# Four interleaved layers on one core: later, two-deep weight loads and a new order for all engines

## The chip, the cores and the metric

One core of a Trainium2 chip runs the kernel. The metric is device time in microseconds of one execution, the median of several runs. TensorE (PE) multiplies, PEld is its weight load, VectorE (DVE), ScalarE (ACT) and GpSimd (POOL) do the elementwise work, SyncE (SP) issues nearly all DMAs.

## The reference

Four layers on x of 2048 tokens by 448 channels: attention A, gated MLP B, A, B, with the same weights in both rounds, bf16 at the ends.

```python
def _A_ref(x, wqkv, wo):            # H=16, Dh=28, W=8, dil=2
    q, k, v = qkv of x @ wqkv
    idx = pos[:, None] - off[None, :]          # the token and 7 before it, 2 apart
    logits = einsum("bhsd,bhswd->bhsw", q, k[idx]) * Dh ** -0.5   # idx < 0 masked
    return softmax(logits) weighted v[idx], heads joined, @ wo
def _B_ref(x, w_gate, w_up, w_down):
    return ((x @ w_gate) * (x @ w_up)) @ w_down                   # F = 1792
x = x + _A_ref(_layernorm(x)); x = x + _B_ref(_layernorm(x))
x = x + _A_ref(_layernorm(x)); x = x + _B_ref(_layernorm(x))
```

## The kernel before

**Tiling.** Tokens lie in 16 blocks of 128, even tokens in blocks 0 to 7 and odd ones in 8 to 15, so that the dilated window becomes a plain one. Layers 0 and 2 are attention, 1 and 3 the MLP. Each layer is cut into chunks of 256 or 512 tokens (`ACH`, `BCH`), and `SEQ` interleaves the chunks of neighbouring layers. All weights are loaded once and stay in SBUF.

**An attention chunk.** Statistics and normalization of a block (`bn`, `mv`, `lnv`, `rstd`, `xn`), then its transposition into `xnTa` (`T`), by TensorE and a copy (`Tps`, in the chunks of `PE_T`) or by a DMA transposition that SP issues. Then the projections into q and k (`qk_chunk`, lines 363 and 740), v (`v_group`), scores (`S`, line 850), `Exp` on ACT (line 857), mask on DVE (line 867), attention times v (`AV`, line 887), normalization and the output projection with `wo` (`Y`). Four of the 16 heads' v goes through DRAM: the projection's spare columns are written to `vt` (SP, line 749) and read back with a DMA transposition (line 760); `vones` fills the rows of ones there.

**A projection unit** is two pieces: in the first, each half of the PE rows works for one of two outputs, in the second the halves are exchanged. The second waits, with a semaphore that TensorE itself raises, for the first to be through (`crossed`, `selfd`). Other pieces may stand between the two.

**An MLP chunk.** Normalization and a DMA transposition into `xnTb` (line 639), 14 gate/up units (`Gps`, `Ups`; each contracts over 7 tiles of 64 channels and depends on all 14 weight tiles `wg` 0 to 6 and `wu` 0 to 6 in `WGU`), the product (lines 978 and 981) and the down projection with `WD` (`Dd`).

**Mixed bursts.** The small matmuls of `S` and `AV` use a part of the PE rows and columns. In the order's text an entry such as `547+415@24.40` puts strips of another, large product (the host) into the burst at the places given.

**The order.** Nothing is decided at run time. `Sched.add` numbers every operation, with its engine choices, dependences and an estimated duration; `ORD` then gives, for each engine, the whole list of operation numbers, and `BANK` the PSUM banks of each. The lists were made by a planner that knew the estimates (`lat` of a DMA: `GUL` for gate and up tiles, `WOL` for wo, `WDL` for the down weights), but `lat` itself has no effect in the built kernel; the dependences and the order do. An engine waits for an operation's semaphores at its place in the list, and everything behind it on this engine waits too. SP is one such list: a DMA that must wait for another one's landing holds up all SP's later DMAs.

**Loads before.** SP issues in order: blocks 0 and 1 of x, two staged parts of wqkv, blocks 2 and 3, the second quarter of x, the third, two tiles of `WV`, the fourth quarter, two small staged tiles (`stv`, the v columns that go into the spare columns of WQK: `wqp`), the four `wo` tiles (line 570), then the chain of bulk weights (`link`): each entry depends on the landing of the entry `DEPTH` places before it, so three are in flight. The chain begins behind the second, third and fourth quarters of x, and goes through the 14 gate/up tiles, `vones` and the four parts of `WD`. Within it stand the transpositions of blocks 14 and 15 of layer 0, behind `wg` 4. ACT issues the other two staged parts of wqkv. The eight staged pieces are copied into `WQK` (`wqk`, line 552): five by POOL, three by ACT. POOL builds the masks `MK` with small selects (line 522) before, between and behind its copies.

The rest of the order around these loads: TensorE warms up on zeros, transposes blocks, projects chunk 0 (q, k), the first v, chunk 1, and so on; the first gate/up unit is its operation 303, and behind the attention chunks the MLP of layer 1 begins, while layer 0's last chunks go on.

Of the kernel before, what the change touches and what calls it, by code (L numbers as in the profile page):

```python
# [22 lines left out]
FC = F // 128  # L23
# [24 lines left out]
GUL = 4000.0  # L48
DEPTH = 3
WOL = 14000.0  # L50
WDL = 3500.0
# [347 lines left out]
def build(nc, A_x, A_wqkv, A_wo, B_w_gate, B_w_up, B_w_down, out):  # L399
# [88 lines left out]

    load_x(0, 0, 1, "d_x0", 3400.0)
    load_x(0, 1, 2, "d_x0b", 4250.0)  # L490
    load_stage("act", 0, 3650.0)
    load_stage("act", 2, 5650.0)
    load_stage("sp", 1, 5850.0)
    load_stage("sp", 3, 6450.0)
    load_x(0, 2, 4, "d_x0h", 7050.0)
    load_x(1, 0, 4, "d_x1", 8300.0)
    load_x(2, 0, 4, "d_x2", 9500.0)
    for a in range(2):
        head_dma("sp", WV[:, 2 * a:2 * a + 2, :], wv_rows(a, 2 * D, 3 * D), ("wv", a), "d_wv", (9650.0, 10850.0)[a])
    load_x(3, 0, 4, "d_x3", 12000.0)  # L500
    for a in range(2):
        head_dma("sp", stage[:, SV + 2 * a * DH * VT:SV + 2 * (a + 1) * DH * VT].rearrange("p (b n) -> p b n", b=2), wv_rows(a, 2 * D + VD, 3 * D), ("stv", a), "d_stv", (11500.0, 12400.0)[a])
    sc.add("act", one(act_table_load), 1650.0, prio=-9900)

    def memset(eng, ap, val, key, est):
        sc.add(eng, one(lambda E: E.memset(ap, val), key), est, prio=-40)

    memset("dve", warm, 0.0, "c_warm", 700)
    memset("dve", eps_sb[:], EPS, "c_eps", 70)
    memset("dve", wo_g[:], 0.0, "c_wo", 1000)  # L510
    sc.add("pool", one(lambda E: E.memset(ident[:], 1.0), "i_id"), 600, prio=-46)
    sc.add("pool", one(lambda E: E.affine_select(ident[:], ident[:], [[-1, 128]], ALU.is_equal, 0.0, base=0, channel_multiplier=1), "c_id"), 300, deps=["i_id"], prio=-46)
# [52 lines left out]
    ones_dst = vt_all.rearrange("(t e) (a n) -> t e a n", e=32, n=128)[:, DH:32]  # L565
    ones_src = ones32[0:32, :].unsqueeze(1).to_broadcast([32, 16, 128])
    for j in range(4):
        dst = wo_g[32 * j:32 * j + DH, :, :]
        src = A_wo.rearrange("(c j e) d -> j e c d", c=4, j=4, e=DH)[j]
        head_dma("sp", dst, src, ("wo", j), "d_wo", WOL, deps=["c_wo"])  # L570
    chain = [("x", -1, 4), ("x", -1, 8), ("x", -1, 12)]

    def link(dst, src, key, sem, lat, deps=()):
        plain_dma("sp", dst, src, key, sem, deps=[chain[-DEPTH], *deps], lat=lat)
        chain.append(key)

    for k in range(7):
        for w, W_ in enumerate((B_w_gate, B_w_up)):
            link(WGU[64 * w:64 * w + 64, k, :], W_[64 * k:64 * k + 64, :], (("wg", "wu")[w], k), f"d_w{'gu'[w]}{k}", GUL)
    link(ones_dst, ones_src, ("vones",), "d_one", WDL, ["c_ones"])  # L580
    for n in range(4):
        f0, f1 = (0, 4, 7, 11, 14)[n:n + 2]
        link(WD[:, f0:f1, :], B_w_down[128 * f0:128 * f1, :].rearrange("(c p) e -> p c e", p=128), ("wd", n), f"d_wd{n}", WDL)
    WDR = [("wd", n) for n in range(4)]
    WO = [("wo", j) for j in range(4)]

# [10 lines left out]
    readersA = {}  # L597
# [110 lines left out]
    def qk_chunk(li, j, prio):  # L708
# [35 lines left out]
        for B in range(c0 // 128, c1 // 128):  # L744
            readersA.setdefault((li, B), []).extend([("Kps", li, j, 3), ("Qps", li, j, 3)])
# [378 lines left out]
```

## Time and profile before

| | before |
|---|---|
| time, median of 3 runs | 384.17 us (384.14 to 384.42) |
| the profiled execution's own time | 383.78 us |
| its span, first to last instruction | 382.0 us |
| granted TensorE clock, mean | 1.00 |
| DVE, ACT, POOL busy share | 70%, 53%, 3% |
| DMA | 22.75 MB, mean 60 GB/s, 272 GB/s in the first slice |
| landing of a gate tile, an up tile (median) | 4.8, 3.5 us |

How to read it: an instruction row gives start and length in us, engine and line, the tiles written and read, the count, and in brackets the idle time of the engine ahead of it with what ended it. `SPq` and `ACTq` are DMA issues; the length is the issue's, the landing comes later. In a row by stages the columns are the stretch, its length, and the busy time of PE, PEld, DVE, ACT and POOL, then the clock, the DMA engines' share and GB/s. Matmuls are pipelined: their rows overlap, and the time that a group holds TensorE is the distance to the next group's start.

### The profile page before, as it was taken

The page shows a single profiled execution, that of the slowest core. Times are in us where ns is not written, and L with a number is a line of the kernel's source. Part 1 is how long each engine was busy: PE and PEld are TensorE (multiplying, and loading weights), DVE is VectorE, ACT ScalarE, POOL GpSimd, SP SyncE. Part 2 cuts the span into 40 slices and gives each one's busy share as a digit, 9 for nine tenths or more (in the row PEclk, how much of TensorE's full clock was granted, in tenths as well). Part 3 has the DMA queues.
Part 4 walks back from the last instruction along what each step waited for, and adds up shares of the span by engine and source line. Part 5 has one row for each costly group of instructions (what it writes and reads, how often), then busy time and mean ns, then how long its engine had stood idle before and what let it go on. Part 6 is the DMA issues. An engine that isn't in the chain of part 4 may idle for free.

```text
span 382.0 us, 14245 instructions
## 1 busy us (share of the span) xinstructions
PE 376.1 (98%) x6406; PEld 211.2 (55%) x6406; DVE 266.5 (70%) x588; ACT 204.3 (53%) x401; POOL 10.1 (3%) x41
## 2 busy tenths in 40 slices
PE   7999999999999999999999999999999999999997
PEld 4556587544555445445566787544455544445764
DVE  6984989996787576786758765764767686454413
ACT  5999976746645773235554555366455453134310
POOL 7110000000000000000000000000000000000000
PEclk9999999999999999999999999999999999999999
DMA  8877532500360044013201115310422004120003
GB/s 272 224 163 204 94 76 47 87 6 2 64 80 15 17 75 64 3 27 61 42 3 29 36 25 90 62 29 9 70 46 22 27 2 94 40 62 2 2 2 108
DMA packets 55615, 22.75 MB, mean 60 GB/s; under 512 B 46132, under 2 KB 54660, under 8 KB 55556
## 3 DMA queue, kind: packets, MB, share of 16 engines
q1 hardware_dynamic: 54868, 21.34, 28.0%
q8 instruction: 50, 0.82, 0.9%
q10 hardware_dynamic: 688, 0.52, 0.4%
q14 instruction: 9, 0.07, 0.1%
HBM read 8.54 MB, written 2.71 MB: 29 GB/s over the span
## 4 chain that ended last, share of the span: by engine, by line
PE 92%; ACT 4%; DVE 1%; DMA 1%; SPq 0%; issue 0%
PE ps L363 84%; PE ps L850 2%; PE ps L366 2%; PE ps L887 2%; PE ps L993 1%; ACT qk L740 1%; DMA x_sb<-in_A_x_dram 1%; DVE st L615 1%; ACT xnTa L654 1%; ACT E_sb L857 0%; SPq L460 0%; ACT R_sb L914 0%; ACT v_sb L832 0%; DVE qk L740 0%; ACT R_sb L913 0%
## 5 line engine op out<-in xcount | busy, mean ns | idle before, releaser
L363 PE MATMUL ps<-xnTb,WGU 64*128 64x512 bf16 (+1 forms) x1914 | 174.2, 333 | 0.0
L363 PEld LDWEIGHTS ps<-xnTb,WGU 64*128 64x128 bf16 x1914 | 93.2, 94 | 70.2 <-issue 0.5
L978 ACT ACTIVATE g_sb<-ps 128x512 bf16<-128x512 f32 (+1 forms) x140 | 69.0, 510 | 84.9 <-PE ps L363 76.9
L981 DVE TENSOR_TENSOR hT<-g_sb,ps 128x512 bf16<-128x512 bf16 (+1 forms) x140 | 77.0, 575 | 51.1 <-ACT g_sb L978 48.5
L363 PE MATMUL ps<-WD,hT 64*128 64x448 bf16 x814 | 84.3, 349 | 0.0
L942 DVE TENSOR_TENSOR x_sb<-x_sb,ps 128x448 bf16<-128x448 bf16 x62 | 36.8, 613 | 39.3 <-PE ps L363 39.2
L363 PEld LDWEIGHTS ps<-WD,hT 64*128 64x128 bf16 x814 | 38.9, 94 | 34.0 <-issue 0.2
L363 PE MATMUL ps<-xnTa,WQK 64*128 64x512 bf16 (+1 forms) x498 | 53.3, 352 | 0.6 <-POOL WQK L552 0.2
L857 ACT ACTIVATE E_sb<-ps 128x1024 bf16<-128x1024 f32 (+1 forms) x36 | 33.9, 980 | 10.7 <-PE ps L850 10.3
L615 DVE BATCH_NORM_STATS2 st<-x_sb 128x6 f32<-128x448 bf16 x64 | 37.6, 615 | 2.0 <-DMA x_sb<-in_A_x_dram 1.4
L636 DVE TENSOR_SCALAR xn_sb<-x_sb,mv,rstd 128x896 bf16<-128x896 bf16 (+1 forms) x64 | 35.4, 571 | 1.3 <-ACT rstd L620 1.2
L363 PEld LDWEIGHTS ps<-xnTa,WQK 64*128 64x128 bf16 x498 | 23.5, 94 | 21.7 <-ACT E_sb L857 0.9
L740 ACT ACTIVATE qk<-ps 128x1024 bf16<-128x1024 f32 (+1 forms) x30 | 27.2, 922 | 6.6 <-PE ps L363 6.4
L363 PE MATMUL ps<-wo_g,oT 64*128 64x448 bf16 x252 | 28.6, 349 | 0.1
L618 ACT ACTIVATE lnv<-mv,eps_sb 128x2 f32<-128x2 f32 (+1 forms) x33 | 9.4, 294 | 34.8 <-DVE mv L617 34.8
L867 DVE TENSOR_TENSOR E_sb<-E_sb,MK 128x1024 bf16<-128x1024 bf16 (+2 forms) x40 | 23.4, 607 | 5.5 <-ACT E_sb L857 5.5
L913 ACT ACTIVATE R_sb<-R_sb 128x480 f32<-128x480 f32 (+1 forms) x34 | 20.3, 604 | 7.3 <-DVE R_sb L912 7.3
L925 DVE TENSOR_TENSOR oT<-O_sb,R_sb 128x480 bf16<-128x480 f32 (+3 forms) x36 | 21.8, 626 | 2.9 <-ACT R_sb L914 2.8
L363 PE MATMUL ps<-WV,xnTa 64*128 64x336 bf16 (+3 forms) x252 | 23.5, 304 | 0.0
L912 DVE STREAM_SHUFFLE R_sb<-O_sb 128x480 f32<-128x480 f32 (+1 forms) x34 | 23.0, 693 | 0.0
L914 ACT ACTIVATE R_sb<-R_sb 128x480 f32<-128x480 f32 (+1 forms) x34 | 20.1, 601 | 0.3
L898 ACT ACTIVATE O_sb<-ps 128x512 f32<-128x512 f32 (+3 forms) x25 | 12.8, 540 | 13.3 <-PE ps L887 13.3
(58 smaller groups left out, 188.7 us busy)
## 6 DMA issues: line engine op xcount, KB each, us to landing
out_dram<-x_sb SPq DMA_DIRECT2D x15, 112.0 KB, 1.8
WGU<-in_B_w_gate_dram SPq DMA_DIRECT2D x7, 224.0 KB, 4.8
WGU<-in_B_w_up_dram SPq DMA_DIRECT2D x7, 224.0 KB, 3.5
x_sb<-in_A_x_dram SPq DMA_DIRECT2D x3, 448.0 KB, 5.9
WD<-in_B_w_down_dram SPq DMA_DIRECT2D x2, 448.0 KB, 3.9
WD<-in_B_w_down_dram SPq DMA_DIRECT2D x2, 336.0 KB, 3.7
vt<-qk SPq DMA_DIRECT2D x42, 16.0 KB
xnTb<-xn_sb SPq DMA_TRANSPOSE x32, 3.0
```

The lines of the kernel that those rows point to most:

```text
L363: return lambda E: E.matmul(out(), lhs(), rhs(), start=start, stop=stop)
L615: sc.add("dve", one(lambda E, B=B: E.bn_stats(st6[:, B, :], x_sb[:, B, :]), ("bn", li, B)), 525.0, deps=[("x", li - 1, B)] + ([("xn", li - ...
L636: sc.add("dve", one(lambda E, B=B, dst=dst, src=src: E.tensor_scalar(dst, src, mv[:, B, 0:1], rstd[:, B:B + 1], ALU.subtract, ALU.mult), ( ...
L740: return E.activation(dst, src, ACT.Copy) if hasattr(E, "activation") else E.tensor_copy(dst, src)
L857: return E.activation(E_sb[:, slot, 2 * hp:2 * hp + 2, 0:w], ps[:, b0:b0 + 2, 0:w], ACT.Exp, scale=SCALE)
L867: return E.tensor_tensor(e, e, m, ALU.mult)
L912: sc.add("dve", one(lambda E: E.stream_shuffle(R_sb[:, rs, 0:w], O_sb[:, os_, 0:w], [DH] * 32), ("Rs", li, qb)), dve_est(w) + 100.0, deps= ...
L913: sc.add("act", one(lambda E: E.activation(R_sb[:, rs, 0:w], R_sb[:, rs, 0:w], ACT.Ln), ("Rl", li, qb)), act_est(w, False), deps=[("Rs", l ...
L925: return E.tensor_tensor(oT[:, :, a % HALF:a % HALF + z - a], O[:, :, a - tok:z - tok], R_sb[:, rs, 0:w].rearrange("p (h n) -> p h n", h=4 ...
L942: sc.add("dve", one(lambda E: E.tensor_tensor(x_sb[:, B, :], x_sb[:, B, :], ps[:, bk[w], 0:D], ALU.add), ("x", li, B)), dve_est(D), deps=[ ...
L978: sc.add("act", one(lambda E, gs=gs, bk=bk: E.activation(g_sb[:, gs, 0:nt], ps[:, bk[0], 0:nt], ACT.Copy), ("G", li, j, fc)), act_est(nt), ...
L981: sc.add("dve", one(lambda E, gs=gs, bk=bk, fc=fc: E.tensor_tensor(hT[:, fc, hs, 0:nt], g_sb[:, gs, 0:nt], ps[:, bk[1], 0:nt], ALU.mult), ...
```

## The change

- The fourth quarter of x is issued behind `WV` and `stv` on SP, and waits for the second tile of `WV` to land.
- The four `wo` tiles wait for that quarter and for the second `stv`.
- The chain of bulk weights begins behind `wo`'s landing and `vones`, and is two deep. `vones` is no longer in the chain but ahead of it.
- The planner's constants for these loads are other ones, and `ORD` and `BANK` are new for all engines and the whole kernel. What the new lists say of the operations that the prediction speaks of: SP has the transposition of block 15 ahead of `wg` 0 and that of block 14 ahead of `wg` 1; `wu` 6 comes ahead of `wg` 6; `wg` 6 stands behind the transpositions of blocks 1 and 0 of layer 1 and two `vt` writes; the parts of `WD` stand among the later `vt` writes and transpositions. POOL makes all eight `wqk` copies and all eight `wqp` copies, and eight small operations of the masks and fills come ahead of the first copy. The first projection of chunk 0 is 201 199 202 200 205 203 (a transposition) 206 204, before 199 200 201 203 202 205 206 204. The first gate/up unit is 300, with the same operations ahead of it as 303 had. `AV` of the query blocks 11 and 12 (547) has no host. On ACT and DVE some 36 copies out of PSUM change the engine.
- Two lists of readers that a later write waits for (`readersA`, `xslot_users`) now name all of a chunk's units, not the last one.

```diff
-GUL = 4000.0
-DEPTH = 3
-WOL = 14000.0
-WDL = 3500.0
+GUL = 2400.0
+DEPTH = 2
+WOL = 2100.0
+WDL = 2400.0
...
-    load_x(3, 0, 4, "d_x3", 12000.0)
+    plain_dma("sp", x_sb[:, 12:16, :], x_par[1][:, 4:8, :], [("x", -1, B) for B in range(12, 16)], "d_x3", deps=[("wv", 1)], lat=2600.0)
...
-        head_dma("sp", dst, src, ("wo", j), "d_wo", WOL, deps=["c_wo"])
-    chain = [("x", -1, 4), ("x", -1, 8), ("x", -1, 12)]
+        plain_dma("sp", dst, src, ("wo", j), "d_wo", deps=["c_wo", ("x", -1, 12), ("stv", 1)], lat=WOL)
+    chain = [("wo", 3), ("vones",)]
...
-    link(ones_dst, ones_src, ("vones",), "d_one", WDL, ["c_ones"])
+    plain_dma("sp", ones_dst, ones_src, ("vones",), "d_one", deps=[("wo", 3), "c_ones"], lat=WDL)
...
-            readersA.setdefault((li, B), []).extend([("Kps", li, j, 3), ("Qps", li, j, 3)])
+            readersA.setdefault((li, B), []).extend([(k, li, j, c) for k in ("Kps", "Qps") for c in range(4)])
...
-        xslot_users[hs] = [("Gps", li, j, FC - 1), ("Ups", li, j, FC - 1)]
+        xslot_users[hs] = [(k, li, j, fc) for k in ("Gps", "Ups") for fc in range(FC)]
```

The SP list up to the first stores, by numbers (78 to 81 are `wo`, 82 to 95 the gate and up tiles in turn, 96 `vones`, 97 to 100 `WD`, 196 and 198 the transpositions of blocks 14 and 15, 297 and 299 those of blocks 0 and 1 of layer 1, 360 to 366, 504 to 510 and 575 to 581 `vt` writes, 514 and 515 and 374, 375, 519, 520 `vt` transpositions):

```diff
-... 9 10 11 12 13 78 79 80 81 82 83 84 85 86 87 88 89 90 196 198 91 92 93 94 95 96 97 98 365 99 361 575 580 299 297 360 510 505 100 508 366 507 363 364 579 509 504 362 506 514 515 374 375 519 520 ...
+... 9 10 12 13 11 78 81 80 79 96 198 82 83 196 84 85 86 87 88 89 90 91 578 93 92 366 363 95 360 299 297 365 361 94 509 510 98 364 576 577 581 97 362 508 505 506 504 579 507 99 580 575 514 100 375 515 374 431 519 ...
```

More of the change, by code (lines that the diff above doesn't have):

```diff
@@ L58 @@
 ORD = {
[5 rows of a table removed]
[5 rows of a table added]
 }
-BANK = "44:1 110:23 114:45 130:01 133:23 136:45 139:23 154:67 157:01 160:23 163:67 178:23 181:23 184:45 187:01 199:67 201:01 203:45 205:23 211:67 215:2367 220:67 228:23 230:45 232:45 234:01 240:01 244:67 248:2345 253:23 265:01 269:4567 274:45 286:23 300:01 303:67 306:23 309:67 312:64 315:56 318:74 321:01 324:01 327:57 330:14 333:64 336:50 339:50 342:12 348:45 350:67 352:23 354:01 367:01 371:01 376:2345 381:45 393:76 397:2301 402:67 414:67 438:20 441:45 444:16 447:03 450:24 453:43 456:41 459:75 462:15 465:63 468:63 471:60 474:32 477:47 480:45 486:64 492:67 494:01 496:67 498:23 511:23 516:45 521:4567 526:23 538:20 542:6745 547:01 559:01 563:67 565:01 567:45 569:23 582:67 587:23 592:6701 597:67 609:23 613:6701 618:01 630:24 654:57 657:52 660:34 663:45 666:37 669:02 672:01 675:46 678:07 681:61 684:30 687:20 690:17 693:62 696:36 702:17 728:67 730:01 732:45 734:67 747:23 751:01 756:4567 761:45 769:2345 774:45 786:45 810:50 813:12 816:64 819:51 822:56 825:67 828:01 831:45 834:30 837:67 840:53 843:42 846:67 849:01 852:67 858:50 884:23 886:01 888:67 890:45 903:23 908:23 913:0145 918:01 930:12 934:4523 939:23 951:01 965:01 968:67 971:04 974:74 977:23 980:73 983:46 986:65 989:40 992:16 995:73 998:42 1001:75 1004:23 1007:25 1023:45 1026:01 1029:67 1032:20 1035:20 1038:01 1041:31 1044:31 1047:45 1050:67 1053:04 1056:36 1059:74 1062:63 1065:30 1093:67 1095:67 1097:23 1099:45 1112:01 1117:45 1122:4567 1127:67 1139:32 1143:6701 1148:67 1160:01 1184:12 1187:45 1190:12 1193:24 1196:52 1199:34 1202:45 1205:34 1208:67 1211:52 1214:35 1217:74 1220:26 1223:23 1226:23 1234:54 1262:01 1264:67 1266:67 1268:01 1281:01 1286:67 1291:01 1296:6701 1301:67 1313:72 1317:6701 1322:67 1334:01 1338:0167 1343:45 1355:47 1379:36 1382:72 1385:34 1388:01 1391:12 1394:56 1397:01 1400:36 1403:13 1406:45 1409:27 1412:07 1415:27 1418:63 1421:61 1429:50 1457:51 1460:26 1463:26 1466:23 1469:50 1472:03 1475:20 1478:74 1481:47 1484:61 1487:32 1490:74 1493:47 1496:32 1499:71 1507:53 1525:15 1528:75 1531:04 1534:36 1537:23 1540:60 1543:62 1546:15 1549:71 1552:47 1555:46 1558:04 1561:02 1564:40 1567:2 1570:6 1573:0"
@@ new lines @@
+BANK = "44:2 110:01 114:45 130:23 133:23 136:23 139:01 154:45 157:67 160:67 163:45 178:45 181:45 184:01 187:45 199:67 201:23 203:01 205:45 211:45 215:2345 220:23 228:23 230:01 232:01 234:67 240:67 244:67 248:4501 253:45 265:23 269:6745 274:01 286:23 300:45 303:56 306:67 309:14 312:27 315:35 318:46 321:01 324:37 327:75 330:50 333:46 336:14 339:63 342:56 348:01 350:23 352:01 354:67 367:23 371:23 376:6701 381:45 393:24 397:0123 402:01 414:23 438:74 441:74 444:64 447:56 450:57 453:32 456:63 459:42 462:20 465:01 468:06 471:13 474:13 477:54 480:20 486:13 492:01 494:23 496:45 498:67 511:45 516:23 521:6701 526:67 538:57 542:0123 547:01 559:02 563:45 565:23 567:67 569:01 582:23 587:45 592:6745 597:67 609:23 613:4567 618:67 630:40 654:20 657:13 660:10 663:67 666:45 669:71 672:20 675:16 678:51 681:04 684:67 687:04 690:23 693:23 696:56 702:23 728:23 730:67 732:45 734:01 747:45 751:67 756:4501 761:23 769:6723 774:67 786:45 810:17 813:54 816:04 819:60 822:51 825:45 828:54 831:23 834:57 837:23 840:65 843:67 846:02 849:43 852:52 858:72 884:45 886:23 888:01 890:67 903:67 908:23 913:0123 918:01 930:61 934:6701 939:45 951:67 965:46 968:03 971:67 974:43 977:16 980:20 983:40 986:01 989:63 992:62 995:60 998:73 1001:71 1004:23 1007:32 1023:71 1026:01 1029:06 1032:01 1035:52 1038:04 1041:76 1044:04 1047:76 1050:70 1053:01 1056:46 1059:51 1062:75 1065:01 1093:45 1095:45 1097:01 1099:45 1112:67 1117:23 1122:0145 1127:23 1139:67 1143:6745 1148:23 1160:45 1184:42 1187:45 1190:67 1193:35 1196:16 1199:45 1202:10 1205:35 1208:74 1211:76 1214:27 1217:53 1220:64 1223:26 1226:73 1234:26 1262:45 1264:45 1266:23 1268:23 1281:23 1286:01 1291:01 1296:2301 1301:45 1313:14 1317:0145 1322:45 1334:60 1338:0145 1343:45 1355:54 1379:46 1382:37 1385:01 1388:63 1391:72 1394:20 1397:25 1400:13 1403:06 1406:71 1409:70 1412:54 1415:16 1418:32 1421:26 1429:14 1457:50 1460:53 1463:13 1466:57 1469:05 1472:13 1475:53 1478:07 1481:62 1484:56 1487:24 1490:62 1493:25 1496:40 1499:72 1507:05 1525:74 1528:47 1531:56 1534:14 1537:02 1540:01 1543:46 1546:63 1549:57 1552:13 1555:46 1558:13 1561:06 1564:01 1567:1 1570:7 1573:4"
```

10 rows, old and new, of the table ORD are left out of this document.

## The prediction

> **What bounds the kernel now.** I read the page first, then the busy time by stage, then TensorE's own order in time, then SP's.
>
> ```profile
> span 382.0 us, 14245 instructions
> PE 376.1 (98%) x6406; PEld 211.2 (55%) x6406; DVE 266.5 (70%) x588; ACT 204.3 (53%) x401; POOL 10.1 (3%) x41
> PE 92%; ACT 4%; DVE 1%; DMA 1%; SPq 0%; issue 0%
> ```
> ```profile
> 7.20:14.40 7.20, 6.85 (x150) 4.59 (x152) 7.12 (x19) 6.25 (x18) 3.98 (x18) 1.00 1.12 319
> 14.40:22.80 8.40, 7.83 (x186) 4.04 (x188) 7.50 (x25) 8.00 (x20) 1.41 (x6) 1.00 0.63 163
> 22.80:39.00 16.20, 16.10 (x401) 9.31 (x398) 10.02 (x23) 15.65 (x27) 0.00 (x0) 1.00 0.79 178
> 80.00:373.50 293.50, 293.50 (x4602) 160.09 (x4596) 196.16 (x418) 138.97 (x271) 0.00 (x0) 1.00 0.21 36
> ```
>
> The columns are the stretch, its length, then PE, PEld, DVE, ACT, POOL busy, clock, DMA share, GB/s. From 80 us to the last stage TensorE has no idle time at all, at full clock. A new order can gain nothing there, it can only open a gap. What the chain that ended last has of ACT, DVE and DMA must lie ahead of that; there TensorE idles 0.35 + 0.57 + 0.10 us in the first three rows, 1.0 us together (matmul ends are modelled, so short stalls between pipelined matmuls come on top). That is what the head has to give, apart from its start.
>
> ```profile
> 7.20 3.71 PE L363 MATMUL ps<-xnTa,WQK 64*128 64x256 bf16 x56 [0.19 <-POOL WQK L552]
> 10.79 0.29 PE L646 MATMUL ps<-ident,xn_sb 64*128 64x64 bf16 x8
> ...
> 14.36 3.06 PE L363 MATMUL ps<-xnTa,WQK 64*128 64x512 bf16 x26 [0.16 <-ACT xnTa L654]
> ...
> 20.72 0.28 PE L646 MATMUL ps<-ident,xn_sb 64*128 64x64 bf16 x8
> ...
> 22.12 0.70 PE L850 MATMUL ps<-qk 28*64 28x64 bf16 x64 [0.57 <-DVE WQK L560]
> 22.76 0.61 PE L363 MATMUL ps<-xnTa,WQK 64*128 64x512 bf16 x4
> ```
> ```profile
> 50.42 1.70 PE L363 MATMUL ps<-xnTb,WGU 64*128 64x256 bf16 x28
> ```
>
> Four dates matter: 7.20 (first projection), 14.36, 22.76 (first projection of chunk 2) and 50.42 (first gate/up unit, which needs all 14 weight tiles). Whatever delays the last goes one to one to the end, since TensorE is full behind it.
>
> **The change part by part.** Besides the loads, the orders of all engines and the bank table are replaced, so I go along TensorE's path.
>
> *Start.* All eight wqk copies now stand on POOL (before: five, three on ACT), and eight small mask operations more stand ahead of the first copy.
>
> ```profile
> 2.63 0.25 POOL L522 TENSOR_SCALAR_AFFINE_SELECT hT<-hT 128x72 bf16<-128x72 bf16 x1
> 3.99 1.06 POOL L552 COPY WQK<-hT 128x448 bf16<-128x448 bf16 x2 [1.12 <-DMA hT<-in_A_wqkv_dram]
> 8.40 1.91 POOL L522 TENSOR_SCALAR_AFFINE_SELECT hT<-hT 128x72 bf16<-128x72 bf16 x9
> 21.05 1.41 POOL L560 COPY WQK<-hT 128x64 bf16<-128x64 bf16 x6 [9.81 <-PE ps L646]
> ```
>
> A select steps by 1.91/9 = 0.21 us, a copy by 0.53. The eight run from 2.85 to about 4.5. Then copy (0,1), one select, and copies (2,0), (0,0), (1,0), (2,1), (3,0), the last of the four that the first unit needs: 4.5 + 6 x 0.53 + 0.21 = 7.9. So the first projection starts near 8.05, 0.85 later than 7.20. Against that, its parts are reordered so that no second half follows its own first half. Before, 56 matmuls took 7.20 to 10.79, 3.59 us, where 28 pairs at 0.11 need 3.06: 0.5 us of waiting, which I put down to those neighbours. It goes: 8.05 + 3.06 + 0.1 (a transposition now in between) = 11.2, and 0.4 is left. ACT, freed of three copies, then reaches the evictions sooner; adding up its steps and TensorE's along the new order, with the durations they had before, I get the end of chunk 1's projections at about 20.6 where before they ended at 20.7, with the stalls before 14.36 used up. Then POOL does all eight wqp copies after it: 20.6 + 0.35 + 8 x 0.235 = 22.85 for the first projection of chunk 2. Taken: +0.1 against 22.76. Bounds: +0.85 if nothing is won back; -0.75 if the late start is recovered in full and the 0.57 and 0.16 stalls go too.
>
> *x and output weights held back.* The last quarter of x waits for WV's second half.
>
> ```profile
> 4.29 1.16 SPq L460 DMA_DIRECT2D WV<-in_A_wqkv_dram  x2
> 8.17 1.87 SPq L460 DMA_DIRECT2D wo_g<-in_A_wo_dram  x4
> 24.02 0.38 DVE L636 TENSOR_SCALAR xn_sb<-x_sb,mv,rstd 128x512 bf16<-128x512 bf16 x1
> ```
> ```profile
> WV<-in_A_wqkv_dram SPq DMA_DIRECT2D x2, 224.0 KB, 6.0
> WD<-in_B_w_down_dram SPq DMA_DIRECT2D x2, 448.0 KB, 3.9
> x_sb<-in_A_x_dram SPq DMA_DIRECT2D x2, 112.0 KB, 2.8
> v_sb<-vt SPq DMA_TRANSPOSE x27, 2.5
> ```
>
> WV lands at 4.9 + 6.0 = 10.9; 448 KB at WD's 3.9 puts x at 14.9. Its first reader (the statistics of block 14) is due at about 15.1 by DVE's new order, so it is hidden; each us beyond that would stall DVE with block 9's normalization behind it. The four wo issues (1.87) wait for x and run to 16.9; with landing and the ones transfer SP is free at about 20. wo is read after 36 us: nothing.
>
> *Bulk weights.* In SP's new order the transposition of block 15 stands ahead of all gate and up weights. xn 15 was ready at 24.4 (24.02 + 0.38); in the new DVE order it stands earlier, behind block 10's, and I estimate 20.9 (its rstd cannot be much before 20, since ACT makes it behind two evictions). A transposition holds SP for 1.3 us, so weight 1 goes at 22.3, where before the weights followed the wo tiles directly, and block 14's stands between weights 2 and 3.
>
> ```profile
> DMA to landing us min/median/max: 3.2/4.6/6.5
> ```
> ```profile
> 43.43 3.74 SPq L639 DMA_TRANSPOSE xnTb<-xn_sb  x2
> 49.37 3.55 SPq L749 DMA_DIRECT2D vt<-qk  x10
> 54.65 8.19 SPq L760 DMA_TRANSPOSE v_sb<-vt  x6
> ```
>
> With three in flight a WGU tile took 4.6 in the median. Two of the same streams would take 2/3 of it, 3.1, and the smallest row is 3.2; I take 3.3. Bounds: 2.8 (half the bytes took that) and 4.6. Then weight 3 goes at 25.8 and the up tile 6 at 26.3 + 5 x 3.3 = 42.8, still ahead of what follows.
>
> The gate tile 6 does not stand there. It stands behind the transpositions of blocks 1 and 0 of layer 1 and two vt writes; behind it are queued the remaining vt writes, WD and the vt transpositions. Block 1's normalized x is ready where the first row above begins, 43.43; the same chain of work (output projection, x, statistics) leads to it, so it shifts as TensorE does: +0.1. So 43.5 + 3.74 (the pair, as measured) + 2 x 0.36 (a tenth of 3.55) = 48.0, and 3.3 to land: 51.3. TensorE is ready for the first gate/up unit at 50.42 + 0.1 = 50.5. It waits 0.75 us. Bounds: pair 2 x 1.3 (8.19/6 is 1.37) and landing 2.8 give 49.6, no wait; landing 4.6 gives 52.6, and writes half as long again 52.9, a wait of 2.4. No other work can cover it: behind the unit TensorE's list goes on in order.
>
> *Later.* The rows of TensorE's order on which this part rests:
>
> ```profile
> 65.20 1.50 PE L363 MATMUL ps<-WD,hT 64*128 64x448 bf16 x14
> ...
> 68.52 0.68 PE L887 MATMUL ps<-E_sb,v_sb 64*32 64x64 bf16 x64
> 69.14 0.60 PE L363 MATMUL ps<-WV,xnTa 64*128 64x336 bf16 x6
> ...
> 77.41 0.28 PE L887 MATMUL ps<-E_sb,v_sb 64*32 64x64 bf16 x24
> ...
> 78.20 0.55 PE L363 MATMUL ps<-wo_g,oT 64*128 64x448 bf16 x4
> ```
>
> WD is first read at 65.2. Its last quarter now comes behind gate tile 6, nine or more vt writes at 0.36, WD's third quarter and one vt transposition: issued near 57 to 58, landed by 62 at 3.9. The vt transposition that the last attention burst ahead of the 65.2 row needs starts near 59 and lands (2.5) near 61.5: hidden, with about 1 us to spare; behind it on SP stand the transpositions for the second gate/up chunk, first read after 73.
>
> One burst of attention matmuls no longer has a host. Alone it holds TensorE 69.14 - 68.52 = 0.62; hosted 78.20 - 77.41 = 0.79, of which two steps of 448 columns are the host's (0.11 x 448/256 = 0.19 each): 0.41. Price +0.2. Thirteen others stay hosted, with about as many cuts.
>
> *At no cost.* The longer write-after-read lists ask for matmuls that stand earlier on TensorE than the wait's next use by several units; the cover is the work of the next chunk, and without it a transposition would wait at most one unit of 0.75 us. In the tail TensorE's three last pieces change places with the same matmuls; SP has four more stores to issue there but x of blocks 10 and 11 is ready one piece earlier, so the last store is still the one that ACT issues.
>
> **Sum.** +0.1 (head), +0.75 (wait for the gate tile), +0.2 (burst without host) = +1.05 on the profiled execution's 383.78, 384.8. That execution is 0.39 under the median of 384.17; on the median it is 385.2.
>
> **Rivals.**
> 1. *Weights hidden.* The last tile lands by 50.5: the pair takes 2.6 or a tile with few others takes 2.8. For it: no row shows the tile with only one other in flight. Against it: no WGU row under 3.2. Time 384.17 + 0.1 + 0.2 = 384.5.
> [...]
> 2. *Faster: the head gains.* If ACT's relief takes the self-waits and the stalls at 14.36 and 22.12 out and the late start is recovered, TensorE is 0.75 earlier at 22.76; block 1's transposition is then earlier too, and with 2.6 and 2.8 the tile lands at 48.9, ahead of 49.7. With the burst, -0.55; with ACT less tight between 23 and 39 (15.65 of 16.20 busy before) it is another 0.5, -1.05 in all. Time 383.1. It decides only if both the pair and the tile are near their lower bounds. Against it: POOL's 0.85.
> 3. *The chain itself is late.* At 4.6 per tile, or with xn 15 at 24.4 as before, the up tile 6 goes at 46 to 49 instead of 42.8, and it stands ahead of the pair. At 47: pair from 47.9, gate tile 6 at 52.4, landed 55.7: a wait of 5.2, time 389.7. For it: the median of 4.6 itself; against it: that was with three in flight.
>
> **How the numbers follow.** Chances: forecast 0.52, rival 1 0.27, rival 2 0.13, rival 3 0.08. The predicted time is the forecast's, 385.2. Its own range is 384.6 to 386.9 (wait 0.15 to 2.4). The range reaches down to most of rival 2 and leaves out rival 3: 383.4 to 387.1. About 0.2%, 0.8 us, is what a measurement can tell here from no change. Slower by more: 0.46 of the forecast, all of rival 3, a little of rival 1: 0.58. Faster by more: rival 2, 0.12. Same: 0.30.
>
> **What would show it.** The first projection starting near 8.0 behind a POOL copy; the first WGU issue behind 22 us; the last gate tile issued at 47 to 49 behind the transpositions into xnTb; a gap on TensorE ahead of the first matmul on xnTb,WGU, which then stands at 51 to 52; none from 80 us to the last stage. Wrong would be: that matmul at 50.4 or earlier; the last WGU tile landed before it with time to spare; new gaps behind 80 us; or a TensorE idle near 62 waiting for a vt transposition.

## The result and the profile after

| | before | after |
|---|---|---|
| median in the comparison | 384.15 us (384.02 to 384.79, 6 runs) | 387.26 us (386.54 to 392.65, 6 runs) |
| ratio, 95% interval | | 1.008 [1.0054, 1.0107] |
| profiled execution's own time | 383.78 us | 386.69 us |
| its span | 382.0 us | 384.9 us |
| mean granted clock of the six runs | 1.000 | 1.000 three times, 0.996 twice, 0.991 once |

By the ratio the change makes the kernel slower by 3.1 us, where 1.0 was forecast. Three runs (392.65 here, and below 391.46 of the place alone and 438.62 of two deep in the kernel before) were in a slower state, and the ratios leave them out. The median of 387.26 counts all six runs; the three at a clock of 1.000 took 386.54 to 386.69, 2.5 us more than before.

The page of the changed kernel: the span, the busy shares, the chain that ended last by engine, and the first group with idle time.

```profile
span 384.9 us, 14247 instructions
PE 376.9 (98%) x6400; PEld 216.1 (56%) x6400; DVE 267.5 (69%) x590; ACT 199.8 (52%) x394; POOL 11.8 (3%) x46
PE 89%; DMA 3%; DVE 3%; POOL 2%; SPq 1%; ACT 1%; issue 0%; POOLq 0%
L363 PE MATMUL ps<-xnTb,WGU 64*128 64x512 bf16 (+1 forms) x1920 | 175.7, 334 | 2.9 <-DMA WGU<-in_B_w_gate_dram 2.9
```

Before, the chain was 92% TensorE and 1% DMA; now 3% of it are DMA. The gate/up group, which had no idle time ahead of it, has 2.9 us. By stretches (columns as before):

```profile
22.70:39.00 16.30, 16.23 (x404) 9.40 (x404) 11.27 (x27) 15.51 (x26) 0.00 (x0) 1.00 0.63 142
39.00:54.00 15.00, 12.10 (x302) 6.58 (x300) 11.83 (x26) 11.93 (x19) 0.00 (x0) 1.00 0.56 140
54.00:80.00 26.00, 25.72 (x602) 17.70 (x600) 23.22 (x55) 16.78 (x36) 0.00 (x0) 1.00 0.51 103
80.00:376.50 296.50, 296.50 (x4694) 166.92 (x4691) 200.13 (x425) 139.35 (x275) 0.00 (x0) 1.00 0.21 34
```

TensorE idles 2.9 us between 39 and 54, 0.3 between 54 and 80, and not at all from 80 to the tail. So all the idle time lies ahead of 80 us. TensorE's own order there:

```profile
8.20 2.36 PE L363 MATMUL ps<-xnTa,WQK 64*128 64x256 bf16 x40 [0.48 <-POOL WQK L552]
...
22.68 1.47 PE L363 MATMUL ps<-xnTa,WQK 64*128 64x512 bf16 x12
...
49.02 0.93 PE L363 MATMUL ps<-wo_g,oT 64*128 64x448 bf16 x8
52.86 0.94 PE L363 MATMUL ps<-xnTb,WGU 64*128 64x256 bf16 x14 [2.90 <-DMA WGU<-in_B_w_gate_dram]
...
65.80 0.26 PE L887 MATMUL ps<-E_sb,v_sb 64*32 64x64 bf16 x17 [0.28 <-DMA v_sb<-vt]
```

The group at 49.02 holds TensorE for some 0.76 (eight steps of 0.095, as the same pieces do a few lines on), so it is free at 49.8. That is 0.6 earlier than the 50.42 of before; and it starts at 52.86, held up for 3.07. The second stall follows at 65.80. The group ahead of it starts at 65.14 and holds TensorE for 0.31 (62.45 to 62.76 in the trace of both edits below, which has no stall there), so the stall is 0.35, of which the view names 0.28. SP's list shows why:

```profile
10.87 0.37 SPq L460 DMA_DIRECT2D x_sb<-in_A_x_dram  x1
...
21.57 0.58 SPq L460 DMA_DIRECT2D WGU<-in_B_w_gate_dram  x1
22.19 0.59 SPq L460 DMA_DIRECT2D WGU<-in_B_w_up_dram  x1
...
40.70 0.47 SPq L460 DMA_DIRECT2D WGU<-in_B_w_up_dram  x1
...
43.85 0.47 SPq L460 DMA_DIRECT2D WGU<-in_B_w_up_dram  x1
44.37 0.48 SPq L749 DMA_DIRECT2D vt<-qk  x1
44.89 3.08 SPq L639 DMA_TRANSPOSE xnTb<-xn_sb  x2
48.02 0.82 SPq L749 DMA_DIRECT2D vt<-qk  x2
48.88 0.48 SPq L460 DMA_DIRECT2D WGU<-in_B_w_gate_dram  x1
```

The up tile 6 goes at 43.85, the pair of transpositions at 44.89, the gate tile 6 at 48.88. Its landing, and the normalized blocks that the pair reads:

```profile
L460 SPq DMA_DIRECT2D WGU<-in_B_w_gate_dram x1: 476/476/476, 48.9 to 48.9; - x1
...
DMA to landing us min/median/max: 3.9/3.9/3.9
```
```profile
41.74 0.73 DVE L636 TENSOR_SCALAR xn_sb<-x_sb,mv,rstd 128x896 bf16<-128x896 bf16 x1
```

48.88 + 3.93 = 52.81. The first of the two blocks was ready at 42.47, but SP stood in its list ahead of the transposition until 44.89, because it waited for a landing before it could issue the up tile 6.

The second stall hangs on the same tile. The chain that ended last has behind it:

```profile
52.83 4.86 DMA WD<-in_B_w_down_dram
...
61.93 3.83 DMA v_sb<-vt
```

The first part of `WD` is linked to the landing of the gate tile 6, the third part to that of the first, and the `vt` transpositions stand on SP behind the third part. It went at 57.71; the transposition that TensorE waits for went at 61.93 and landed at 65.76.

### The profile page after: what moved, and what is told of

Its sections match the earlier page's. It is cut to its first block, busy times and chain, and to the rows that moved or that the text cites. A ratio compares the mean times of both kernels' runs of the same rounds, so it can differ in the third digit from the quotient of the medians.

```text
span 384.9 us, 14247 instructions
## 1 busy us (share of the span) xinstructions
PE 376.9 (98%) x6400; PEld 216.1 (56%) x6400; DVE 267.5 (69%) x590; ACT 199.8 (52%) x394; POOL 11.8 (3%) x46
## 4 chain that ended last, share of the span: by engine, by line
PE 89%; DMA 3%; DVE 3%; POOL 2%; SPq 1%; ACT 1%; issue 0%; POOLq 0%
PE ps L363 82%; PE ps L850 2%; PE ps L366 2%; PE ps L887 2%; PE ps L993 1%; DMA WD<-in_B_w_down_dram 1%; DMA WGU<-in_B_w_gate_dram 1%; DMA v_sb<-vt 1%; POOL WQK L552 1%; POOL hT L522 1%; SPq L760 1%; ACT qk L740 1%; DVE E_sb L867 0%; SPq L749 0%; DVE xn_sb L636 0%
## 5 line engine op out<-in xcount | busy, mean ns | idle before, releaser
L363 PEld LDWEIGHTS ps<-xnTb,WGU 64*128 64x128 bf16 x1920 | 96.7, 94 | 72.5 <-DMA WGU<-in_B_w_gate_dram 3.3
L363 PEld LDWEIGHTS ps<-WD,hT 64*128 64x128 bf16 x806 | 40.3, 94 | 31.2 <-issue 0.2
L867 DVE TENSOR_TENSOR E_sb<-E_sb,MK 128x1024 bf16<-128x1024 bf16 (+2 forms) x40 | 23.2, 608 | 7.2 <-ACT E_sb L857 7.0
L363 PEld LDWEIGHTS ps<-wo_g,oT 64*128 64x128 bf16 x256 | 12.4, 94 | 10.8 <-PE ps L363 0.5
```

The costliest lines, as they stand in the source:

```text
L363: return lambda E: E.matmul(out(), lhs(), rhs(), start=start, stop=stop)
L867: return E.tensor_tensor(e, e, m, ALU.mult)
```

## The experiments

The theory after reading this: the wait is made by two things together, the **place** of the gate tile 6 (behind the pair and two writes on SP) and the **pace** of the chain (two deep, so that SP is late already at the up tile 6). The rivals: one of them alone does it; or the head's late start does.

**Place alone.** The changed kernel with the gate tile 6 ahead of the pair:

```diff
-... 95 360 299 297 365 361 94 509 ...
+... 95 360 94 299 297 365 361 509 ...
```

> The changed kernel with one entry moved in SP's list: gate tile 6 stands ahead of the two transpositions into xnTb instead of behind them and two vt writes. Theory 'place': the tile is issued near 44.9 us (it waits for gate tile 5 to land, 44.8) and lands near 48.4; the pair moves back by about 0.5 and now ends last, landed near 50.2; the first gate/up matmul at 50.0 to 50.4 instead of 52.85, and the vt transposition ahead of the attention at 65 us comes in time: 383.7 to 384.2 us, clock 1.0 in all runs. Rival 'pace' (two in flight are too slow wherever the tile stands): the first gate/up matmul stays behind 51.5, 385.3 us or more.

Measured: 387.12 us median of 12 runs, ratio to before (384.95) 1.006 [1.0026, 1.0093]. Six of the 12 runs had a mean clock of 0.996 or 0.991 (388.3 to 391.5); the six at 0.999 or 1.000 took 384.97 to 385.94. SP and TensorE in its trace:

```profile
44.87 0.47 SPq L460 DMA_DIRECT2D WGU<-in_B_w_gate_dram  x1
45.38 2.64 SPq L639 DMA_TRANSPOSE xnTb<-xn_sb  x2
```
```profile
50.42 0.94 PE L363 MATMUL ps<-xnTb,WGU 64*128 64x256 bf16 x14 [0.42 <-DMA xnTb<-xn_sb]
```

The stall shrinks to 0.42 and its releaser is another one: now the pair, pushed back to 45.38, lands last. But the second stall, which was expected to go, grows from 0.28 to 0.81:

```profile
PE ps L887 <- DMA v_sb<-vt: 0.8, 1, 0.8
```

So the expected time and the expected clock were missed. The place alone takes away most of the wait at the first unit, but at full clock only some 1.0 us of the time (385.6 in the middle of the six runs, against 386.6).

**Pace alone.** The changed kernel with three in flight:

```diff
-DEPTH = 2
+DEPTH = 3
...
-    chain = [("wo", 3), ("vones",)]
+    chain = [("stv", 1), ("wo", 3), ("vones",)]
```

> The changed kernel with the chain of bulk weights three deep, lists unchanged. Theory 'pace': up tile 6 goes near 41.5 us instead of 43.85, SP is free when block 1's normalized x is ready (42.5), the pair follows at once, gate tile 6 is issued near 46.7 and lands near 50.5; TensorE, ready at 49.8, waits 0.7 us instead of 3.07: about 384.2 us. Theory 'place' alone (the tile's place behind the pair costs the whole wait): it is issued no earlier than 48, wait 2.5 us or more, 386 us.

Measured: 385.54 us (384.72 to 386.96, 12 runs, all clocks 0.999 or 1.000), ratio 1.0018 [1.0001, 1.0035].

```profile
42.85 0.47 SPq L460 DMA_DIRECT2D WGU<-in_B_w_up_dram  x1
...
43.89 3.02 SPq L639 DMA_TRANSPOSE xnTb<-xn_sb  x2
...
47.82 0.48 SPq L460 DMA_DIRECT2D WGU<-in_B_w_gate_dram  x1
```
```profile
51.25 0.94 PE L363 MATMUL ps<-xnTb,WGU 64*128 64x256 bf16 x14 [0.79 <-DMA WGU<-in_B_w_gate_dram]
```

The up tile 6 is 1.00 earlier, the gate tile 6 1.06, and the wait for it falls from 2.90 to 0.79. Only half of this fall is the earlier issue: the tile also came 0.55 faster in this execution (the unit starts 3.43 behind the tile's issue, for 3.98), and TensorE came to the unit 0.5 later (its group before starts at 49.53 for 49.02). The second stall grows here too:

```profile
PE ps L887 <- DMA v_sb<-vt: 1.1, 1, 1.1
```

So the expected 384.2 was missed, and the pace alone also wins some 1.0 us (385.5 against 386.6).

**Both edits together**, place and pace, as in the two diffs above.

> Both edits: three deep, and gate tile 6 ahead of the pair. If place and pace together are the whole of the wait: no gap ahead of the first gate/up matmul, which stands at 49.8 to 50.0 us (0.5 ahead of the kernel before), and 383.4 to 383.8 us, a little faster than before. If the late start of the weights is a cause of its own: a gap of 0.5 us or more is left and the time is at or above 384.2.

Measured: 383.85 us (383.37 to 384.69, 12 runs, all at 1.000), ratio 0.9967 [0.995, 0.9983].

```profile
42.42 0.47 SPq L460 DMA_DIRECT2D WGU<-in_B_w_gate_dram  x1
42.94 2.76 SPq L639 DMA_TRANSPOSE xnTb<-xn_sb  x2
```
```profile
50.27 0.93 PE L363 MATMUL ps<-xnTb,WGU 64*128 64x256 bf16 x14
```

No wait is left at the first gate/up unit, and the list of TensorE's waits has no DMA in it: the stall for `v_sb` is gone as well, since everything behind the tile on SP comes earlier. Each edit alone won some 1.0 us, both win 2.8 (386.6 to 383.85), as the second stall goes only with both. With both edits the kernel is faster than the one before. So the changed order as such is worth about 1 us by the medians (the two kept traces, with spans of 381.9 and 382.0, hardly differ), and the late tile takes back more than that.

**Host restored.** The same with `415` as a host in the burst of query blocks 11 and 12:

```diff
-... 547!v 415!p ...
+... 547+415@24.40!v ...
```

> The changed kernel three deep, with gate tile 6 ahead of the pair, and with the attention burst of query blocks 11 and 12 hosting the output projection's second half again, as in the kernel before. The host's price is 0.2 us: the burst and what follows hold TensorE 0.2 us less, and the time is 0.2 under the run with both edits (383.85 median there, on its chip). If the hosting gives nothing, the milestones behind 78 us stay as they were.

Measured: 383.55 us (383.04 to 386.27, 12 runs), ratio to before (384.9) 0.9969 [0.995, 0.9988]; spans of the two profiled executions 381.3 and 381.9. In the traces the burst and what is left of `415` hold TensorE for 1.19 with the host (76.87 to the next gate/up product at 78.06) and for 1.38 without it (77.38 to 78.76): 0.19, as forecast. But at the next output projection (81.22 and 81.78) 0.14 of this is lost again, and 0.5 of the 0.6 between the spans was there ahead of the burst. So the 0.3 between the medians, which the intervals do not tell from nothing, is not shown to be the host's. By its median this version is, with the last one below, the fastest.

**The gap filled.** The changed kernel with 48 extra matmuls on constants ahead of the first gate/up unit, so that TensorE waits busy:

```diff
+    fb = Banks(2)
+    fins = [(lambda E: E.matmul(ps[:, fb[0], 0:128], ident[:], ones32[:], start=True, stop=True), None) for _ in range(48)]
...
+    sc.add("pe", fins, 0.0, deps=["c_id", "c_ones"], mode="F", acquire=fb, release=[(fb, 0), (fb, 1)])
```

> The changed kernel with 48 small matmuls (128 columns, 2.7 us) that multiply constants into the two banks of the first gate/up unit, ahead of its wait; the output doesn't use them. Theory 'clock': the 3.07 us gap is what lets the granted clock fall in some runs (0.996 and 0.991 in three of six); with TensorE busy there all runs have clock 1.0 and lie within 0.2 us of 386.6. Rival: the scatter has another cause, and runs at 387.8 and above with a clock under 1.0 appear as before.

Measured: 389.65 us (388.51 to 391.23, 6 runs), ratio 1.012 [1.0091, 1.0149], all clocks 0.999 or 1.000.

```profile
50.03 2.85 PE L1063 MATMUL ps<-ones,ident 128*128 128x128 bf16 x48
52.82 0.94 PE L363 MATMUL ps<-xnTb,WGU 64*128 64x256 bf16 x14
```
```profile
PE ps L887 <- issue: 1.5, 1, 1.5
```

The unit starts where it did, so the filler costs nothing there, and no run's clock fell. The time missed the expectation: other stalls appeared, the longest of 1.5 us behind 286.8, for which the profile shows no releaser. What makes them is not settled. The runs also still scatter, by 2.7 us at full clock, so the clock is not the only cause of scatter.

**The change once more, unaltered.**

> The changed kernel itself, on the same chip as the next three. 386.5 to 386.9 us where the clock stays at 1.0. Theory 'clock' (a TensorE gap of about 3 us can let the clock fall): some runs show a mean clock of 0.996 or 0.991 and are 1 to 5 us longer. Rival (those runs were a chance of one chip): no run under 0.999.

Measured: 388.04 us (386.55 to 389.01, 6 runs), ratio to before (384.9) 1.0082 [1.0059, 1.0105]; one run at 1.000 (386.55), the others at 0.996 and 0.991. The kept trace is one at 0.996. Its granted clock is 0.50 from 53.09 to 56.50; this stretch, with one of the same length on either side:

```profile
49.67:53.09 3.42, 0.99 (x16) 0.51 (x14) 1.66 (x4) 2.09 (x3) 0.00 (x0) 1.00 0.65 174
53.09:56.50 3.41, 3.41 (x30) 1.96 (x28) 1.18 (x3) 0.88 (x2) 0.00 (x0) 0.50 0.53 153
56.50:59.92 3.42, 3.42 (x68) 3.00 (x64) 3.06 (x9) 2.16 (x6) 0.00 (x0) 1.00 0.45 110
```

After the wait TensorE is granted half its clock for 3.41 us: 30 matmuls, where the next stretch of the same length has 68. The wait, and what follows it, in the first trace of the change:

```profile
49.00:52.80 3.80, 0.96 (x20) 0.31 (x8) 2.16 (x6) 2.43 (x3) 0.00 (x0) 1.00 0.60 140
52.85:56.50 3.65, 3.64 (x62) 2.95 (x64) 1.88 (x5) 2.02 (x5) 0.00 (x0) 1.00 0.57 164
```

There the gap is longer (3.07 by the distance of the groups; in the trace at 0.996 it is 2.60, from 49.96 to 52.56), and yet the clock behind it is 1.00, with 62 matmuls in 3.65 us. What decides between the two is not shown. The traced run at 0.996 is still only 0.9 us longer than the first trace of the change (387.58 for 386.69), as the tile came 0.3 earlier and the slowed TensorE did not have to wait for `v_sb`.

**The chain's head.** The changed kernel with block 15's transposition behind the first two weight tiles instead of ahead of them:

```diff
-... 79 96 198 82 83 196 ...
+... 79 96 82 83 198 196 ...
```

> The changed kernel with one entry moved in SP's list: the transposition of block 15 stands behind the first two weight tiles instead of ahead of them. Theory 'late start': the first tile is issued near 19.3 us instead of 21.6, the chain stays two deep and ends 2.2 us earlier (up tile 6 near 41.6), the pair starts when block 1's x is ready (42.5), gate tile 6 goes near 46.5 and lands near 50.3: TensorE waits 0.5 us instead of 3.07, about 384.1 us. Rival 'pace': the saved time is lost again to transfers beside each other, and the wait stays over 1.5 us, 385.2 or more.

Measured: 387.94 us (386.07 to 388.44, 6 runs), ratio 1.0064 [1.0039, 1.0089]. The expectation missed: the first tile goes 2.0 earlier, but the second waits for the landing of `vones`, and by the up tile 6 the lead is gone (43.97, in the changed kernel 43.85).

```profile
19.55 0.56 SPq L460 DMA_DIRECT2D WGU<-in_B_w_gate_dram  x1
21.46 0.47 SPq L460 DMA_DIRECT2D WGU<-in_B_w_up_dram  x1
```

Two of the six runs had a clock of 1.000 (386.07 and 386.37). The profiled one, at 0.996, shows the half clock again (0.50 from 54.31 to 57.73), behind 3.41 us in which TensorE was idle for 2.25:

```profile
50.90:54.31 3.41, 1.16 (x20) 0.90 (x22) 0.62 (x2) 1.24 (x3) 0.00 (x0) 1.00 0.60 153
54.31:57.73 3.42, 3.42 (x32) 2.28 (x30) 2.05 (x5) 1.56 (x4) 0.00 (x0) 0.50 0.57 162
```

**Two deep in the kernel before**, nothing else changed (`DEPTH = 2`):

> The kernel before with DEPTH = 2 alone, its lists unchanged. Theory 'two deep costs only where the chain ends late': the chain starts at 10 us here and the last gate tile, before at 33 us, lands near 38; the transpositions of blocks 14 and 15 behind gate tile 4 move back some 3 us but are read first at 39 us; no gap ahead of the first gate/up matmul at 50.4: the same as before within 0.4 us. Rival 'pace': two deep is dear by itself, slower by 1 us or more.

Measured: 389.13 us median of 6 runs, five of them from 388.29 to 389.70 at a clock of 0.995 or 0.996, ratio 1.0109 [1.0089, 1.0129]. No cost was expected. The one kept trace is that of 438.62 us, at a mean clock of 0.852. TensorE's longest wait there:

```profile
PE ps L363 <- DMA xnTa<-xn_sb: 1.6, 1, 1.6
```

In that kernel's SP list the transpositions of blocks 15 and 14 of layer 0 stand behind the gate tile 4. They are read near 31 us, not late in layer 0 as I had taken it, and two deep brings SP to them at 27.1 instead of 23.2. Part of the 4.2 us is the lower clock of the five runs (0.4 or 0.5% of 384, some 1.5 to 1.9 us, an estimate). To see the pace without that wait, the same with the two moved up behind the gate tile 3:

```diff
-... 88 89 90 196 198 91 ...
+... 88 196 198 89 90 91 ...
```

> The kernel before with two in flight, and the transpositions of blocks 15 and 14 moved ahead of gate tile 4, so that the slower chain does not make them late. Theory: the pace alone costs nothing where the chain starts at 10 us: last weight landed near 40, no wait on a weight and no wait on xnTa near 31 us: 384.2 to 384.9, clock 1.0. Rival: two in flight cost by themselves (389.1 us with the transpositions in their old place): 386 or more.

Measured: 384.75 us (383.98 to 387.89, 11 runs, one of them at 0.996), before 384.57, ratio 1.0008 [0.999, 1.0026].

```profile
37.38 0.47 SPq L460 DMA_DIRECT2D WGU<-in_B_w_up_dram  x1
```

The last of the 14 tiles goes at 37.4, nearly fourteen us ahead of its reader at 51.2. So two in flight by themselves cost nothing that these runs can tell; they cost what is queued behind them on SP, where that is due.

**Holding back alone in the kernel before**, three deep (the same two transpositions moved ahead, so that they keep their time):

```diff
-... 10 11 12 13 78 79 80 81 82 83 84 85 86 87 88 89 90 196 198 91 ...
+... 10 12 13 11 78 79 80 81 82 83 84 85 86 87 196 198 88 89 90 91 ...
...
+    plain_dma("sp", x_sb[:, 12:16, :], x_par[1][:, 4:8, :], [("x", -1, B) for B in range(12, 16)], "d_x3", deps=[("wv", 1)], lat=2600.0)
...
+        plain_dma("sp", dst, src, ("wo", j), "d_wo", deps=["c_wo", ("x", -1, 12), ("stv", 1)], lat=WOL)
```

> The kernel before, three in flight, with only the last quarter of x and wo held back (and the transpositions of blocks 15 and 14 ahead of gate tile 3, so that they do not come later). Theory: holding back alone costs nothing; x lands near 14.7 us, the first weight goes near 16.5, three each 4.6 us end the 14 tiles near 40, ten us ahead of the first gate/up unit at 50.4: 384.2 to 384.9, clock 1.0, no wait of TensorE on a weight. Rival: the later quarter of x stalls VectorE at the statistics of blocks 12 to 15, and everything behind it: 385 or more, with a wait of VectorE on x near 14 us.

Measured: 388.08 us (386.44 to 389.54, 6 runs, three of them at 0.996), ratio to before (384.57) 1.009 [1.0065, 1.0115]. The rival was right:

```profile
14.71 2.21 DVE L615 BATCH_NORM_STATS2 st<-x_sb 128x6 f32<-128x448 bf16 x4 [2.52 <-DMA x_sb<-in_A_x_dram]
```
```profile
18.74 0.82 PE L363 MATMUL ps<-xnTa,WQK 64*128 64x512 bf16 x6 [1.99 <-ACT v_sb L832]
```

VectorE's old order reads the quarter at 12.2; it lands at 14.7, and the 2.5 us pass through ACT to TensorE, which stands still for 1.99; the end is 2.1 later. The weights themselves were in time. In the changed kernel the same DMA, landing at the same date, makes no wait, as VectorE's new order first reads the quarter at 14.99.

**An earlier start.** The version with the host, with POOL's eight mask operations behind or between its first copies, and these in another order:

```diff
-... 34 35 22 28 29 25 38 31 32 63 39 66 62 64 67 68 69 40 65 41 ...
+... 34 63 62 35 28 66 64 68 67 69 65 22 29 25 38 31 32 39 40 41 ...
```

> The changed kernel with the gate tile ahead of the transpositions, three in flight, the host back in the burst, and on POOL the eight mask operations behind the first copies and the copies of first halves (k, 0) first. Theory: the first projection starts near 7.65 us instead of 8.20, and 0.3 to 0.55 us of it reach the end: 383.0 to 383.3. Rival: the late start is won back before 22 us in any case (ACT and DVE set the pace there): no change against 383.55.

Measured: 384.31 us (383.44 to 385.13, 11 runs), before 384.57, ratio 0.999 [0.9978, 1.0003]. VectorE and TensorE:

```profile
15.83 0.63 DVE L615 BATCH_NORM_STATS2 st<-x_sb 128x6 f32<-128x448 bf16 x1 [1.23 <-DMA x_sb<-in_A_x_dram]
```
```profile
7.41 2.36 PE L363 MATMUL ps<-xnTa,WQK 64*128 64x256 bf16 x40 [0.32 <-ACT xnTa L654]
...
17.42 0.29 PE L646 MATMUL ps<-ident,xn_sb 64*128 64x64 bf16 x8 [0.59 <-DVE xn_sb L636]
```

The start is 0.7 earlier than with the host alone (8.15), and then VectorE comes to the held-back quarter of x before it has landed (at 15.8, after 5.0 us in this execution). The lead is lost in this trace: the first projection of chunk 2 stands at 23.06, with the host alone at 22.63. The expected gain was missed. In the changed kernel, and with the quarter held back in the kernel before, this transfer took 3.8 us, so it need not take 5.0, and what took the lead in the other runs is not shown.

**An earlier start and an earlier quarter.** The last run gives that quarter its old place again, without the wait for `WV`:

```diff
-... 9 10 12 13 11 ...
+... 9 10 11 12 13 ...
...
-    plain_dma("sp", x_sb[:, 12:16, :], x_par[1][:, 4:8, :], [("x", -1, B) for B in range(12, 16)], "d_x3", deps=[("wv", 1)], lat=2600.0)
+    load_x(3, 0, 4, "d_x3", 12000.0)
```

> As the run before (POOL's masks behind the first copies), and the last quarter of x issued in its old place, not held back. Theory: in that run VectorE waited 1.23 us at 14.6 us for this quarter, landed at 15.81, and it is this wait that took back the earlier start; with x landed near 12.4 the first projection stands at 7.45 and chunk 1 ends 0.5 to 0.8 earlier than in the version with the host (383.55): 382.8 to 383.2. Rival: WV and the two staged tiles now land later behind that quarter (10.9 and 13.1 in the kernel before), TensorE waits at the first v group near 11, and nothing is won: 383.5 or more.

Measured: 383.4 us (382.87 to 384.84, 12 runs, all at 1.000), before 384.37, ratio 0.998 [0.9968, 0.9992]. VectorE's wait is gone, but at 22.41 the first projection of chunk 2 stands only 0.2 earlier than with the host alone. The theory's mechanism held, its gain did not: against 383.55 on another chip nothing can be told.

## Why the prediction was wrong in size

The direction was forecast, and the place: a TensorE that waits at its first gate/up unit for the gate tile 6, in a kernel without idle time behind it. The step that failed is the term **"wait for the gate tile", 0.75 with an upper bound of 2.4; it measured 3.07** in the profiled execution, and 2.60 in the second kept trace of the same kernel.

- **When TensorE is ready.** Forecast 50.5, measured 49.8. The head's bill (+0.1) was right up to chunk 2 (22.85 forecast, 22.68 measured, with the first projection at 8.20 for 8.05), in part by luck: 22.85 was the end of POOL's `wqp` copies, which were through at 22.24, and it was the scores ahead of the projection, waiting 0.24 for ACT, that set the date. By 50 us the new order had won 0.6 in this execution (in the other kept traces without the earlier start TensorE was ready between 49.8 and 50.3). Each us that TensorE is early is a us more of waiting for a transfer that does not depend on it: a gain of the head counts as a loss in this term. This is 0.7 of the difference.
- **When the pair begins.** Forecast 43.5, from the date of its input; measured 44.89, though the input was there at 42.47. I had the up tile 6 at 42.8 and did not ask what SP does between it and the pair. It went at 43.85: one of the first two tiles took 4.9 us to land, so that the second up tile went at 27.12 for 26.3, and the five steps from there were 3.35 each for 3.3. A write stands in between as well. The pair itself was shorter than the 3.74 of before (3.08). Together the tile was issued at 48.88 instead of 48.0, 0.9 of the difference. Three in flight take this back (up tile 6 at 42.85, gate tile 6 at 47.82).
- **How long the tile takes.** 3.93 for 3.3, 0.6 of the difference (an estimate from the unit's start is 3.4 with the pace alone, and 3.6 in the second trace of the change). The three make 0.75 + 2.2, 2.95 of the 3.07.
- **"Hidden, with about 1 us to spare"** was said of the `vt` transpositions. They were not: a stall of 0.35 at 65.80. Forecast were a start near 59 and a landing after 2.5; the one that TensorE waited for went at 61.93 and took 3.83, behind a part of `WD` that hung on the late tile. The 1 us to spare was less than the error of the dates that it was reckoned from.
- **The clock.** The sum took the granted clock to stay at 1.00. In 8 of 12 runs of the changed kernel it did not. The runs at 1.000 took 386.54 to 386.69, and the medians of the two sets are 387.26 and 388.04: this is 0.6 to 1.5 us that no term had.
- **What held.** x's last quarter hidden (landing 14.65, first read 14.99, so 0.34 to spare); the first WGU issue behind block 15's transposition (21.57 for 22.3); the burst without its host (0.2 forecast, 0.19 at the burst itself, most of it gone a few us later); no idle time from 80 us on.

Of the rivals, "weights hidden" needed a tile of 2.8 us or a pair of 2.6. The pair measured 3.08 and the tile 3.93. The smallest landing of a gate or up tile that this trace has, with two in flight, is 3.1. "The chain itself late" put the up tile 6 at 47 and the end at 389.7; it was the right mechanism with too late a date. "The head gains" had TensorE 0.75 earlier at 22.76, where it was 0.1; yet with the tile out of the way the new order is about 1 us faster by the medians (0.9967 with both edits). Its condition, that the tile not wait, is the one that failed.

## What to carry to other kernels

A transfer that stands behind waiting instructions on its queue inherits all their delays: date it from the queue (what issues last ahead of it, and what that waits for), not from its own chain or from its neighbours' inputs. Here the pair's input was there at 42.47, SP came to the pair at 44.89, and the tile behind it went at 48.88. Where a faster stretch leads up to a transfer with a fixed date, its gain turns into waiting time (here 0.6 of the 3.07); so price a wait with the reader early and the transfer late at once. A load can be slowed or held back for nothing, and the same edit costs 2 us or more in another order (slowed: ratios of 1.0008 and 1.0109; held back: no wait in the changed kernel, 2.52 us of VectorE's in the kernel before): the cover belongs to the order, not to the load.

## What the runs showed of the hardware

In two traces a wait of TensorE cost more than its length. Behind 3.42 us in which it was busy for only 0.99 (the change once more), and behind 3.41 with 1.16 (the chain's head), the granted clock was 0.50 for the next 3.41 and 3.42 us. At half clock such a stretch loses 1.7 us of work (an estimate from these two figures); the runs of the change at 0.996 took 1.0 to 2.4 us more than those at 1.000. But in the first trace of the change, with a wait of 3.07 for 2.60, the clock stayed at 1.00, and what decides it is not shown. The same kernel took 386.5 to 386.7 in the four of its 12 runs at 1.000, and 387.6 or more in the eight at 0.996 or 0.991. A mean clock of 0.991 would be two such stretches (an estimate: 2 x 3.41 x 0.5 of 386 is 0.9%); no trace of such a run was kept. With the gap filled by useless matmuls no run's clock was under 0.999 (6 runs), nor with the gap removed (12 runs with both edits, 12 with the host); with it 8 of 12 were, and in the kernel before with 1.99 us of waiting 3 of 6. It also fell, rarely, where no trace shows such a gap: to 0.996 in one of 29 runs of the kernel before.

What stays open is the kernel with the place alone: six of its 12 runs had the lower clock (0.996 or 0.991), and its one trace, from a run at 1.00, shows no gap that long (behind the start, 1.0 at most).
